# Decay attention and a gated projection on one core: other offsets of a list scheduler's priorities

## The chip, the cores and the metric

The kernel runs on 1 core of one Trainium2 chip. The metric is the device time of one execution in microseconds (us); a row of runs is told by its median. Three runs of the kernel before took 592.39, 594.8 and 597.3 us, the median is 594.8 us.

## What is computed

Eight batches of eight heads, 576 positions, head width 64. The result of the attention, heads side by side, is the x (576 x 512 for a batch) of a gated projection.

```python
scores = q @ k.T / sqrt(64)
cum    = cumsum(log(clip(f, 1e-4, 1)))
scores = where(causal, -1e9, scores + cum[:, None] - cum[None, :])
attn   = softmax(scores)                    # 1e-9 is added to the row sums
x      = attn @ v                           # heads side by side: 576 x 512 a batch
gate   = sigmoid(sum(conv_w[k] * x shifted by 4 - k rows, k = 0..4))
out    = (gate * (x @ w_val)) @ w_out
```

q, k, v and f are float32; the three weights are float64, which the kernel takes as pairs of 32-bit words and splits itself into a high and a low float part.

## The kernel before

**Units of work.** The 64 heads are done as 32 pairs i = 0..31, two heads in one unit, four pairs to a batch. A pair goes through these steps, and each step has a class name in the planner, which the text below uses:

- load, dec: DMAs of q, k, v and of the decay rows (tiles dm and dl); sel (L428, L431): GpSimd sets the causal part in them.
- T(i,q), T(i,k), T(i,z) (L524, L531): TensorE transposes q, k and the last 64 positions of both (z) into PSUM. The first four pairs copy the result as it is (TF, tile Xf, which lies in the tile named gate); from pair 4 on it is split into a high part (TH, tile Xh, L369) and a low part (TL, tile Xl, L515, always VectorE).
- S(i,...) (L354): the score products, in three groups. S(i,0) and S(i,1) fill four and two PSUM banks with rows 0 to 511 of both heads, S(i,z) fills two banks with rows 512 to 575. A group needs both parts of its transposes.
- red (L598): VectorE adds the decay in place and takes the row minimum; SX (L602): ScalarE takes the exponential into P or Pl and the row sums; rec (L611, L612): VectorE takes their reciprocals; norm: P or Pl is scaled, on GpSimd or VectorE (L376) or ScalarE (L374).
- PT (L643, L661, L662): TensorE transposes P, one unit for each head and group of row blocks; PT(i,l) is that of Pl. Copies bring the results into pt (L369).
- PV(i,0), PV(i,1) (L354, pt with vt): the products with v. Their result is copied to x (L369), and from x come xh (L369) and xl (L712), the two parts of x for the projection, and the five taps of the gate's convolution (conv: L376 or L374 for the first, L724 for four).

At the end of a batch follow sig (L740: sigmoid of the gate over 2304 columns, with a table load before and after it on ScalarE), Mv (x times w_val), H (L769), hh and hl (the two parts of the product), Mo(b,t) (times w_out, row block t of batch b) and O, OD (copy to ot and store). Each product of split operands is three matmuls. The eight blocks of 128 rows of the two weights, wv0 to wv3 and wo0 to wo3, are loaded into ot or wu and decoded during pairs 1 to 7 by some nine steps for each block: L822 to L834 on ScalarE and VectorE, a copy of the high part (L369 into wall) and a product for the low part (L862 into wall), which VectorE or GpSimd may do.

**What sets the order.** No order is written by hand. `plan_t`, `plan_s`, `plan_pt`, `plan_pv`, `plan_moe`, `plan_w` and `load` hand nodes to the class `Plan`: a class, the engines that may do the work with an assumed duration for each, what is read and written, and a base priority that is the pair's number plus a fraction. `Plan.add` adds to it OFF[class][phase], where the phase is 0 to 5 by the base priority (limits 0.95, 3, 6, 11, 28). `Plan.order` then simulates the engines with these durations: it takes the node that can start first (on an engine of several, its start plus PEN[class, engine][phase]), among those that can start at the same time the lowest priority. On TensorE a node of the same row layout as the one before is preferred by STICK. A node that needs PSUM takes from 8 banks the first that is free (`seize`, `room`), and a bank comes free when its last reader is done. What comes out is one fixed order of instructions for each engine and one fixed owner after another for each bank; on the chip the engines follow it with semaphores. So a number in the three tables moves an instruction on its own engine, gives an instruction to another engine, or gives a step another PSUM bank, and with it another predecessor to wait for.

## Time and profile before

| | |
|---|---|
| three runs | 592.39, 594.8, 597.3 us, median 594.8 |
| the profiled execution | 592.27 us, of it 590.5 us span from the first to the last instruction |
| TensorE busy | 558.2 us, 95% of the span |
| VectorE, ScalarE, GpSimd busy | 461.3, 447.9, 249.9 us |
| mean granted TensorE clock | 0.977 |
| DMA | 93.43 MB, 158 GB/s on average |

The profile is that of one execution. Its first part gives the busy time of each engine: PE is TensorE's matrix products, PEld its weight loads (which lie beside the products), DVE is VectorE, ACT ScalarE, POOL GpSimd, SP the queue that issues DMAs. Its second part cuts the span into 40 slices of 14.8 us. A row of a timeline gives the start, the time from the first start to the last end, the engine, the line in the kernel, the operation with the tile written and the tiles read, and how many instructions the row holds; in brackets stands the idle time of the engine ahead of the row and what ended it. A row of the windows gives a stretch and the busy time of PE, PEld, DVE, ACT and POOL in it, then the granted clock, the share of the DMA engines' time and GB/s. A row of the groups by line gives the count, then the busy time and the mean duration of one in ns, then the idle time ahead.

### The profile page before, as it was taken

To read this page: it belongs to the slowest core of one execution; us is meant where nothing else is said; L and a number is where in the kernel's file an instruction comes from. 1 tells how busy PE (TensorE), PEld (TensorE's weight loads), DVE (VectorE), ACT (ScalarE), POOL (GpSimd) and SP (SyncE) were. 2 spreads that over 40 slices of the span, in tenths; PEclk is the share of its full clock that TensorE was granted. 3 is DMA by queue.
4 is the path that set the end of the run, shared out by engine and by line. 5 is a ranking of instruction groups with operands and counts; after the bars stand their busy time and mean duration, and the time that the engine had idled before them with its cause. 6 is when DMAs were issued, how large, how long until landed. Compare 5 with 4: busy or idle time off the path is not lost.

```text
span 590.5 us, 14025 instructions
## 1 busy us (share of the span) xinstructions
PE 558.2 (95%) x4693; PEld 487.5 (83%) x4693; DVE 461.3 (78%) x1238; ACT 447.9 (76%) x1217; POOL 249.9 (42%) x398
## 2 busy tenths in 40 slices
PE   8778898799889999999999999999999999999997
PEld 7546587689779998889989988899888987889885
DVE  6488979899988797788967897668879789587660
ACT  4688878999878887888887988677798876764511
POOL 3431367334322556456553746455556461210200
PEclk9779699899999999999999999999999999999999
DMA  6979898676465585757866675466776544220012
GB/s 147 266 185 266 170 240 230 166 196 168 114 183 135 143 234 158 188 136 188 188 157 167 184 189 154 117 179 152 193 201 188 159 120 123 80 83 19 37 37 89
DMA packets 136294, 93.43 MB, mean 158 GB/s; under 512 B 118474, under 2 KB 118494, under 8 KB 136222
## 3 DMA queue, kind: packets, MB, share of 16 engines
q1 hardware_dynamic: 136142, 92.52, 59.0%
q8 instruction: 37, 0.61, 0.4%
q14 instruction: 35, 0.29, 0.2%
q10 hardware_dynamic: 80, 0.02, 0.0%
HBM read 82.60 MB, written 9.91 MB: 157 GB/s over the span
## 4 chain that ended last, share of the span: by engine, by line
PE 69%; DVE 13%; DMA 8%; ACT 5%; issue 3%; SPq 1%; POOL 1%; DVEq 0%; POOLq 0%; ACTq 0%
PE banks L354 54%; PE banks L643 9%; DVE banks L598 6%; PE banks L524 3%; DMA wu<-in_moe_w_val_dram 3%; ACT P L602 3%; DMA dm<-decd 2%; DVE gate L724 2%; PE banks L661 2%; DMA qn<-in_q_dram 1%; DVE negm L598 1%; SPq L381 1%; DMA kn<-in_k_dram 1%; PE banks L531 1%; ACT P L374 1%
## 5 line engine op out<-in xcount | busy, mean ns | idle before, releaser
L602 ACT ACTIVATE P<-banks,negm 128x256 f32<-128x256 f32 (+3 forms) x256 | 131.9, 531 | 35.9 <-DVE negm L598 35.6
L369 ACT COPY pt<-banks 128x256 f32<-128x256 f32 (+2 forms) x320 | 116.9, 436 | 42.8 <-PE banks L643 36.4
L598 DVE CUSTOM_DVE_ANT_0 banks<-banks,dm 128x256 f32<-128x256 f32 (+3 forms) x256 | 120.4, 515 | 33.4 <-PE banks L354 22.2
L724 DVE SCALAR_TENSOR_TENSOR gate<-x,cw,gate 128x576 f32<-128x576 f32 x128 | 111.6, 876 | 1.7
L354 PE MATMUL banks<-xh,wall 128*128 128x288 f32 x512 | 110.2, 300 | 1.0 <-ACT ot L369 0.7
L428 POOL TENSOR_SCALAR_AFFINE_SELECT dm<-dm 128x256 f32<-128x256 f32 x126 | 57.5, 481 | 122.0 <-DMA dm<-decd 100.1
L376 POOL TENSOR_SCALAR P<-P,rz 128x128 f32<-128x128 f32 (+3 forms) x132 | 79.0, 614 | 56.5 <-DVE rz L612 32.7
L643 PE MATMUL banks<-ident,P 128*128 128x128 f32 x640 | 93.2, 283 | 9.3 <-POOL P L376 4.1
L354 PE MATMUL banks<-pt,vt 128*64 128x128 f32 (+2 forms) x1408 | 99.0, 294 | 3.2 <-DVE Xl L515 1.9
L354 PEld LDWEIGHTS banks<-pt,vt 128*64 128x64 f32 x1408 | 87.1, 139 | 16.0 <-issue 3.1
L354 PE MATMUL banks<-wall,hh 128*128 128x512 f32 x288 | 92.8, 403 | 2.8 <-ACT P L602 2.6
L643 PEld LDWEIGHTS banks<-ident,P 128*128 128x128 f32 x640 | 74.4, 144 | 20.0 <-POOL P L376 5.3
L354 PEld LDWEIGHTS banks<-xh,wall 128*128 128x128 f32 x512 | 83.8, 188 | 2.8 <-ACT ot L369 1.1
L354 PE MATMUL banks<-xl,wall 128*128 128x288 f32 x256 | 75.4, 294 | 0.0
L712 POOL TENSOR_TENSOR xl<-x,xh 128x576 fp32r<-128x576 f32 x32 | 47.1, 1475 | 46.1 <-ACT xh L369 46.1
L354 PEld LDWEIGHTS banks<-wall,hh 128*128 128x128 f32 x288 | 51.0, 188 | 13.3 <-ACT P L602 3.6
L354 PE MATMUL banks<-Xh 128*128 128x288 f32 (+2 forms) x280 | 59.1, 346 | 1.2 <-DVE Xl L515 1.0
L782 POOL TENSOR_TENSOR hl<-h,hh 128x576 fp32r<-128x576 f32 (+2 forms) x36 | 36.9, 1032 | 48.4 <-ACT hh L369 48.4
L354 PE MATMUL banks<-wall,hl 128*128 128x512 f32 x144 | 56.5, 392 | 0.0
L354 PE MATMUL banks<-Xh,Xl 128*128 128x288 f32 (+2 forms) x280 | 53.6, 315 | 0.0
L354 PE MATMUL banks<-Xl,Xh 128*128 128x288 f32 (+2 forms) x280 | 53.3, 314 | 0.0
L602 ACT ACTIVATION_READ_ACCUMULATOR P<-banks,negm 128x1 f32 x256 | 52.9, 206 | 0.0
(105 smaller groups left out, 916.7 us busy)
## 6 DMA issues: line engine op xcount, KB each, us to landing
dm<-decd SPq DMA_DIRECT2D x62, 640.0 KB, 5.4
out_dram<-ot SPq DMA_DIRECT2D x36, 256.0 KB, 2.1
dl<-decd SPq DMA_DIRECT2D x62, 144.0 KB, 3.8
qn<-in_q_dram SPq DMA_DIRECT2D x64, 128.0 KB, 3.6
kn<-in_k_dram SPq DMA_DIRECT2D x64, 128.0 KB, 5.8
vt<-in_v_dram SPq DMA_DIRECT2D x64, 128.0 KB, 2.9
zn<-in_k_dram SPq DMA_DIRECT2D x32, 32.0 KB, 3.1
vt<-in_v_dram SPq DMA_DIRECT2D x32, 32.0 KB, 3.2
```

The costliest lines, as they stand in the source:

```text
L354: nc.tensor.matmul(out, lhsT=lhsT, rhs=rhs, start=start, stop=stop)
L369: (eng.copy if eng is nc.scalar else eng.tensor_copy)(out=out, in_=in_)
L376: eng.tensor_scalar(out=out, in0=in_, scalar1=col, scalar2=0.0, op0=ALU.mult, op1=ALU.add)
L428: nc.gpsimd.affine_select(out=t, in_=t, pattern=[[0, 2], [-1, P]], base=0, channel_multiplier=1, compare_op=ALU.is_ge, fill=-BIG)
L524: nc.tensor.transpose(out=bank(key)[:, n * P:(n + 1) * P], in_=src[:, n].rearrange("p h d -> p (h d)"), identity=ident)
L598: nc.vector.tensor_tensor_reduce(out=sl, in0=sl, in1=add[:, o:o + ext], op0=ALU.add, op1=ALU.min, scale=-0.125, scalar=3.0e38, accum_out=n ...
L602: nc.scalar.activation(out=dst[:, o:o + ext], in_=bank(key)[:, c0:c0 + ext], func=AF.Exp, bias=negm[r][:, col], scale=-1.0, accum_out=zs[r ...
L643: nc.tensor.transpose(out=bank(key)[:, c:c + P], in_=Pt[m][:, BOFF[b] + P * j:BOFF[b] + P * j + P], identity=ident)
L661: nc.tensor.transpose(out=bank(key)[:, P * j:P * j + P], in_=Pl[r][:, D + P * j:D + P * j + P], identity=ident)
L712: any_("xl", {"POOL": 1.4, "DVE": 0.67}, p, lambda eng: eng.tensor_tensor(out=xl[s], in0=xv, in1=xh[s][:, :].bitcast(F32), op=ALU.subtract ...
L724: eng.scalar_tensor_tensor(out=gt, in0=src, scalar=wt_, in1=gt, op0=ALU.mult, op1=ALU.add)
L782: eng.tensor_tensor(out=hl[jj][:, y:y + x1 - x0], in0=h32[:, x0:x1], in1=hh[jj][:, y:y + x1 - x0].bitcast(F32), op=ALU.subtract)
```

## The change

STICK goes from 18.18 to 16.65, and nearly all numbers of the tables OFF and PEN change; all steps, durations, buffers and dependencies stay. The new numbers come from the same kind of search as the old ones, with disturbances of the assumed durations half as large. Some rows of the diff:

```diff
-STICK = 18.18
+STICK = 16.65
...
-    ... "T": (25.97, 49.19, -30.29, -36.4, -10.95, -19.47),
+    ... "T": (13.33, 44.36, -9.43, -41.78, -1.47, -41.3),
...
-    ("norm", "ACT"): (0.44, 0.25, 1.01, 0.21, 1.1, 2.13),
+    ("norm", "ACT"): (0.0, 0.17, 13.52, 0.11, 0.94, 4.26),
...
+    ("wo", "POOL"): (0.0, 0.0, 0.13, 0.0, 0.0, 0.0), ...
```

What it does to the program, by the orders of the two kernels: the 3941 matmuls are the same, with 160 changes of row layout instead of 159. Of the norms, ScalarE has 118 instead of 100, VectorE 35 instead of 39, GpSimd 135 instead of 149. Of the eight low products of the weights (L862) VectorE has seven instead of four: wv0, wv2 and wo3 come to it from GpSimd. One first conv (pair 4) goes from ScalarE to VectorE, and one copy of a z transpose too. Three places follow that the prediction speaks of; the names at the end of a tile's name are its buffer.

TensorE, pairs 2 to 4 (kn_76 and zn_78 are k and z of pair 5, Pl_86 and the pt tiles those of pair 2, gate_114 the operands of S(3,1)). Before:

```order
L643 MATMUL banks<-ident,P_84 128x128 x4
L524 MATMUL banks<-ident,kn_76 128x128 x4
L354 MATMUL banks<-gate_114 128x384 x2
L354 MATMUL banks<-gate_114 128x128 x2
L643 MATMUL banks<-ident,P_85 128x128 x4
L531 MATMUL banks<-ident,zn_78 128x128 x2
L661 MATMUL banks<-ident,Pl_86 128x128 x4
L662 MATMUL banks<-ident,Pl_86 64x128
L354 MATMUL banks<-pt_89,vt_91 64x128
```

Now, from the last product of PV(2,0) on:

```order
L354 MATMUL banks<-pt_90,vt_91 64x128
L661 MATMUL banks<-ident,Pl_86 128x128 x4
L662 MATMUL banks<-ident,Pl_86 64x128
L524 MATMUL banks<-ident,kn_76 128x128 x4
L531 MATMUL banks<-ident,zn_78 128x128 x2
L354 MATMUL banks<-pt_89,vt_91 64x192
```

PV(2,0), the rows of pt with 64x128, stood behind T(5,k), S(3,1), T(5,z) and PT(2,l); now it stands ahead of T(5,k), T(5,z) and PT(2,l), and right behind S(3,1); PV(2,1), the rows with 64x192, follows T(5,z), and S(4,z), which stood between PV(2,0) and PV(2,1), follows PV(2,1) and the first transposes of pair 3.

TensorE, pairs 3 to 6 (qn_73, kn_75 and zn_77 are q, k and z of pair 6; P_83 and P_85 are P of pair 4, Xh_80 and Xl_82 the operands of S(5,...)). Before, behind S(4,1):

```order
L354 MATMUL banks<-Xl_81,Xh_79 128x128 x2
L524 MATMUL banks<-ident,qn_73 128x128 x4
L524 MATMUL banks<-ident,kn_75 128x128 x4
L531 MATMUL banks<-ident,zn_77 128x128 x2
L643 MATMUL banks<-ident,P_84 128x128 x4
```

Now, inside the products of pair 5:

```order
L354 MATMUL banks<-Xl_82,Xh_80 128x256 x2
L643 MATMUL banks<-ident,P_83 128x128 x2
L643 MATMUL banks<-ident,P_85 128x128 x4
L524 MATMUL banks<-ident,kn_75 128x128 x4
L531 MATMUL banks<-ident,zn_77 128x128 x2
L354 MATMUL banks<-Xh_80 128x384 x2
L354 MATMUL banks<-Xh_80,Xl_82 128x384 x2
```

T(6,k) and T(6,z) stood right behind T(6,q), ahead of PT(3,1,(2,0)); T(6,q) has stayed there, T(6,k) and T(6,z) now follow PV(3,0), PV(3,1), S(5,z), PT(4) and S(5,0).

VectorE, the last weight block wo3 (gate_114 holds the parts being decoded, wu the block; dm_68 and dm_69 are the decay tiles of pair 9). Before:

```order
L832 SCALAR_TENSOR_TENSOR gate_114<-wu 128x512
L834 TENSOR_SCALAR wu<-gate_114 128x512
L369 CAST wall<-gate_114 128x512
L598 ISA banks,negm_94<-banks,dm_68 128x512
L598 ISA negm_94 128x1
L598 ISA banks,negm_94<-banks,dm_69 128x512
```

Now:

```order
L832 SCALAR_TENSOR_TENSOR gate_114<-wu 128x512
L834 TENSOR_SCALAR wu<-gate_114 128x512
L369 CAST wall<-gate_114 128x512
L862 TENSOR_TENSOR wall<-gate_114,wu 128x512
L376 TENSOR_SCALAR gate_114<-x_99,cw 128x576
L376 TENSOR_SCALAR gate_114<-x_100,cw 128x576
L598 ISA banks,negm_94<-banks,dm_68 128x512
```

The low product of wo3 (L862) has come to VectorE, and two first taps of the convolution stand behind it, ahead of the row minima of pair 9.

One more place, in words: on TensorE the first row block of the output product, Mo(0,2) and Mo(0,3) of batch 0 (L354, wall with hh and hl), stood behind PT(8,1,(2,0)) and PT(8,l); now both stand ahead of them, and Mo(0,2) has a bank that PT(8,0,(2,0)) leaves where before it had one that S(9,1) leaves, while Mo(0,3) now has one of S(9,1). On ScalarE the sigmoid of batch 1's gate with its table loads now stands ahead of the pt copies of pair 8.

More of the change, by code (lines that the diff above doesn't have):

```diff
@@ L63 @@
 }
 PEN = {
[4 rows of a table removed]
-    ("X", "DVE"): (10.66, 6.42, 35.96, 35.67, 3.07, 32.37), ("conv", "ACT"): (37.06, 9.53, 0.39, 7.85, 12.52, 8.12),
-    ("conv", "DVE"): (0.01, 0.0, 0.02, 0.0, 0.09, 1.39), ("conv", "POOL"): (51.47, 31.7, 58.49, 34.72, 29.95, 35.69),
-    ("hh", "ACT"): (0.0, 0.0, 0.0, 0.0, 0.5, 3.04), ("hh", "DVE"): (0.0, 0.0, 1.73, 16.52, 3.91, 0.39),
-    ("hl", "DVE"): (0.0, 0.0, 0.45, 0.87, 4.98, 0.0), ("hl", "POOL"): (0.0, 0.0, 0.0, 0.67, 0.0, 30.02),
-    ("load", "ACT"): (1.58, 0.0, 0.0, 0.0, 0.0, 0.0), ("norm", "ACT"): (0.44, 0.25, 1.01, 0.21, 1.1, 2.13),
@@ L74 @@
-    ("norm", "DVE"): (6.2, 19.99, 21.87, 2.29, 2.56, 0.18), ("norm", "POOL"): (0.63, 17.37, 0.04, 25.85, 0.46, 2.15),
-    ("sel", "DVE"): (36.1, 36.18, 41.87, 17.73, 90.83, 1.24), ("sel", "POOL"): (0.65, 0.76, 0.61, 0.6, 1.44, 6.22),
-    ("start", "ACT"): (10.22, 0.0, 0.0, 0.0, 0.0, 0.0), ("start", "DVE"): (4.31, 0.0, 0.0, 0.0, 0.0, 0.0),
-    ("start", "POOL"): (5.56, 0.0, 0.0, 0.0, 0.0, 0.0), ("wo", "ACT"): (0.0, 0.0, 5.81, 0.0, 0.0, 0.0),
[4 rows of a table removed]
[4 rows of a table added]
+    ("conv", "ACT"): (37.96, 19.77, 7.45, 24.88, 23.07, 22.76), ("conv", "DVE"): (0.12, 0.0, 0.02, 0.0, 0.08, 1.2),
@@ new lines @@
+    ("conv", "POOL"): (46.14, 15.26, 57.23, 24.18, 25.57, 24.33), ("cut0", "ACT"): (0.18, 0.0, 0.0, 0.0, 0.0, 0.0),
+    ("hh", "ACT"): (0.0, 0.0, 0.0, 0.0, 0.5, 20.58), ("hh", "DVE"): (0.0, 0.0, 3.69, 4.33, 8.35, 0.06),
+    ("hl", "DVE"): (0.0, 0.0, 0.34, 5.33, 13.61, 0.3), ("hl", "POOL"): (0.0, 0.0, 0.19, 0.21, 0.13, 30.97),
+    ("load", "ACT"): (2.24, 0.0, 0.0, 0.0, 0.0, 0.0), ("norm", "ACT"): (0.0, 0.17, 13.52, 0.11, 0.94, 4.26),
+    ("norm", "DVE"): (11.52, 23.51, 21.54, 13.3, 3.63, 0.16), ("norm", "POOL"): (0.05, 12.7, 0.04, 30.93, 0.45, 2.7),
@@ L82 @@
+    ("sel", "DVE"): (32.07, 32.67, 50.11, 9.42, 80.65, 0.16), ("sel", "POOL"): (1.41, 0.6, 0.06, 0.1, 0.26, 18.53),
+    ("start", "ACT"): (14.6, 0.0, 0.0, 0.0, 0.0, 0.0), ("start", "DVE"): (2.21, 0.0, 0.0, 0.0, 0.0, 0.0),
+    ("start", "POOL"): (3.01, 0.0, 0.0, 0.0, 0.0, 0.0), ("wo", "ACT"): (0.0, 0.0, 16.48, 0.0, 0.0, 0.0),
[4 rows of a table added]
 }
```

10 lines of the change are left out of this document (5 added, 5 removed), and 44 rows, old and new, of tables (OFF, PEN).

## The prediction

> **What bounds the kernel now.** I read the page's first two parts, then the windows by stage, then the waits in the timelines of PE, DVE and POOL, then the chain that ended last.
>
> ```profile
> span 590.5 us, 14025 instructions
> PE 558.2 (95%) x4693; PEld 487.5 (83%) x4693; DVE 461.3 (78%) x1238; ACT 447.9 (76%) x1217; POOL 249.9 (42%) x398
> ...
> PEclk9779699899999999999999999999999999999999
> ```
>
> PE is busy for 558.2 of 590.5 us and does the same 3941 matmuls afterwards. An order alone can win only the 32.3 us in which PE stands still and what PE loses at a lower clock; it can lose without such a limit. The clock row has its low digits in the first eight slices (14.8 us each). Where the idle time lies, the windows tell:
>
> ```profile
> core 0: us, PE busy (x) PEld busy (x) DVE busy (x) ACT busy (x) POOL busy (x), PEclk, DMA share, GB/s
> 15.00:45.00 30.00, 22.00 (x135) 15.57 (x134) 18.77 (x55) 21.51 (x59) 12.59 (x21) 0.77 0.91 226
> 60.00:75.00 15.00, 12.42 (x68) 9.12 (x66) 13.26 (x36) 12.10 (x37) 5.67 (x8) 0.67 0.77 163
> 90.00:170.00 80.00, 70.86 (x612) 61.38 (x611) 75.36 (x199) 72.00 (x195) 33.06 (x47) 0.98 0.63 171
> 170.00:300.00 130.00, 129.50 (x1170) 117.02 (x1169) 106.79 (x288) 109.24 (x300) 65.37 (x106) 1.00 0.68 176
> 300.00:590.00 290.00, 283.44 (x2395) 251.88 (x2394) 211.48 (x562) 200.54 (x538) 115.26 (x170) 1.00 0.47 130
> ```
>
> From 170 us on PE itself is the bound: 0.50 us idle of 130, then 6.56 of 290. Between 90 and 170 us PE is idle for 9.14 us, and DVE, busy for 75.36 of 80, is the bound. Between 15 and 45 us PE is idle for 8.00 us, and the DMA engines are busy at 0.91. Whatever the new order does after 170 us can hardly gain; what it does earlier has to pass DVE or the DMAs.
>
> **The start, pairs 0 and 1 (term A).** GpSimd's norms of pair 0 end PE's longest wait.
>
> ```profile
> 22.29 2.85 PE L643 MATMUL banks<-ident,P 128*128 128x128 f32 x12 [3.45 <-POOL P L376]
> ```
> ```profile
> 21.01 0.77 POOL L428 TENSOR_SCALAR_AFFINE_SELECT dm<-dm 128x256 f32<-128x256 f32 x2 [4.41 <-DMA dm<-decd]
> ```
>
> POOL stood 4.41 us in front of a select that waited for its DMA, with the norms queued behind it; the new order puts two of these norms ahead of the select and gives ScalarE norms of pair 1. At best the whole wait of 3.45 us goes. But the next thing that all else waits for is a weight block, in the chain that ended last:
>
> ```profile
> 39.33 8.42 DMA wu<-in_moe_w_val_dram
> ...
> 54.10 7.02 DMA wu<-in_moe_w_val_dram
> ```
>
> The blocks of 512 KB take 8.42 and 7.02 us while the DMA engines are 0.91 busy, and the second waits for wu until the first is decoded. Work of pairs 0 and 1 that ends earlier then waits longer at 47.75 us. A DMA share of 0.91 is nearest to "no gain": I take 0, bounds -3.45 and 0.
>
> **Pairs 2 to 4 (term B).** The first order fence. DVE's waits here:
>
> ```profile
> 75.77 0.77 DVE L598 CUSTOM_DVE_ANT_0 banks<-banks,dl 128x576 f32<-128x576 f32 x1 [1.25 <-PE banks L354]
> ...
> 78.36 0.52 DVE L376 TENSOR_SCALAR gate<-x,cw 128x576 f32<-128x576 f32 x1 [1.55 <-ACT x L369]
> ...
> 80.22 0.70 DVE L598 CUSTOM_DVE_ANT_0 banks<-banks,dm 128x512 f32<-128x512 f32 x1 [0.49 <-PE banks L354]
> ```
>
> DVE waits 1.25 us for S(4,z), 1.55 us for the x of pair 2 and 0.49 us for S(4,0), 3.29 us together. PE loses this beside them:
>
> ```profile
> 64.56 0.79 PE L524 MATMUL banks<-ident,kn 128*128 128x128 f32 x4 [1.45 <-ACT P L602]
> ...
> 71.51 2.83 PE L354 MATMUL banks<-pt,vt 128*64 128x128 f32 x24 [0.71 <-ACT P L602]
> ```
>
> T(5,k) waits 1.45 us for a PSUM bank that an exponential of pair 3 holds, with everything behind it, and PV(2,0) 0.71 us. With PV(2,0) ahead of T(5,k), its bank from a copy of PT(2), PE has work during the 1.45 us, and PV(2,1), now ahead of S(4,z), brings x earlier: the 1.55 goes. S(4,z) and S(4,0), on the other hand, stand behind more transposes, so the 1.25 and the 0.49 stay or grow. DVE is busy for 13.26 of 15 us in this window, so what it can win is bounded by its waits: bounds -3.3 and 0. About half of the 3.29 belongs to the wait that goes: -1.6.
>
> **Low products, a conv and a cast on DVE (term C).**
>
> ```profile
> L862 POOL TENSOR_TENSOR wall<-gate,ot 128x512 fp32r<-128x512 f32 x3 | 4.0, 1335 | 3.9 <-DVE ot L834 3.9
> L862 DVE TENSOR_TENSOR wall<-gate,wu 128x512 fp32r<-128x512 f32 x3 | 2.1, 684 | 0.0
> ...
> L376 DVE TENSOR_SCALAR gate<-x,cw 128x576 f32<-128x576 f32 x31 | 16.7, 540 | 14.5 <-ACT x L369 14.5
> ```
>
> Three low products at 0.684 us are 2.05 us more for DVE (3 x 1.335 less for POOL, which has 47 of 80 us free), the first conv is 0.54; the cast of a z transpose (0.34 us, row at 90.19 below) and one step of the table's start that goes to ScalarE cancel nearly. Together at most +2.7. wv0 and wv2 fall into stretches in which DVE waits for DMAs (the 1.26 us ahead of 47.77 below) and cost nothing there; wo3 falls between 154 and 156 us in DVE's bound stretch, ahead of pair 9's row minima:
>
> ```profile
> 47.77 0.43 DVE L824 TENSOR_SCALAR gate<-wu 128x512 int32<-128x512 int32 x1 [1.26 <-DMA wu<-in_moe_w_val_dram]
> ```
>
> I take +0.7, the one product that has no cover, bounds 0 and +2.7 (all cover gone).
>
> The Trainium skill speaks against this: "GPSIMD Engine Reference", section "1. Specifications", has GpSimd share its SBUF interface with VectorE, so that VectorE instructions with two SBUF inputs contend with it. These rows show that it matters here:
>
> ```profile
> 155.48 0.69 DVE L598 CUSTOM_DVE_ANT_0 banks<-banks,dm 128x512 f32<-128x512 f32 x1
> ...
> 158.36 7.51 DVE L724 SCALAR_TENSOR_TENSOR gate<-x,cw,gate 128x576 f32<-128x576 f32 x7
> ...
> 167.57 0.81 DVE L724 SCALAR_TENSOR_TENSOR gate<-x,cw,gate 128x576 f32<-128x576 f32 x1
> ```
> ```profile
> 155.31 1.40 POOL L862 TENSOR_TENSOR wall<-gate,wu 128x512 fp32r<-128x512 f32 x1 [3.81 <-DVE wu L834]
> ...
> 161.92 3.34 POOL L712 TENSOR_TENSOR xl<-x,xh 128x576 fp32r<-128x576 f32 x2 [4.93 <-ACT xh L369]
> ```
>
> Seven convs beside two of POOL's xl took 7.51 us where one alone takes 0.81, so 1.84 us were lost in POOL's 3.34. But the row minimum that ran beside POOL's product of wo3 took 0.69 us, as the one at 80.22 did (0.70). By that rule the move would give back up to 1.40 x 1.84 / 3.34 = 0.77 us and term C would be about 0, the sum 0.7 lower; by the row beside this very product there is nothing to give back, and I stay with +0.7.
>
> **Mo(0,2) (term D).**
>
> ```profile
> 167.91 0.72 PE L354 MATMUL banks<-wall,hh 128*128 128x512 f32 x2 [2.40 <-ACT P L602]
> ```
>
> Mo(0,2) waits 2.40 us for a bank that the exponentials of S(9,1) leave, and these wait for DVE, which does the seven convs first (7.51 us, above). Now Mo(0,2) takes a bank that a copy of PT(8,0) leaves, but Mo(0,3) behind it takes one of S(9,1), and PT(8,1) and PT(8,l), now behind both, take banks that T(11,q) and T(11,k) leave; and on ScalarE the sigmoid comes ahead of the copies of PT(8):
>
> ```profile
> 170.05 1.28 ACT L740 ACT_TABLE_LOAD   x1
> 171.35 2.13 ACT L740 ACTIVATE gate<-gate 128x2304 f32<-128x2304 f32 x1
> 173.50 1.28 ACT L742 ACT_TABLE_LOAD   x1
> ```
>
> That is 4.69 us in which no copy for PV(8) is made. So Mo(0,2)'s 1.4 us of work come earlier and the same wait stands in front of Mo(0,3): the bounds are -2.40 and 0, and I take -0.5, near the lower gain since the releaser (S(9,1)) is the same.
>
> **After 170 us (term E).** PE is 99.6% and 97.7% busy there, the reorders of pairs 10 to 30 move work that is covered: 0. The bounds are -2 (of 7.06 us idle) and +2, a wait like that of 2.40 above where a bank's new owner is late. In the last batch the order at the end is the old one.
>
> **The sum.** 0 - 1.6 + 0.7 - 0.5 + 0 = -1.4, by which the profiled execution of 592.27 (span 590.5, 1.8 around it) would take 590.9. That execution was 2.5 us below the median of the three runs shown; against it the forecast is 594.8 - 1.4 = 593.4 us. 1% of the median, about what a measurement of this kernel can tell from no change, is 5.9 us: faster means below 588.9, slower above 600.7.
>
> **Rival 1, faster: the early clock comes back.** Between 60 and 75 us the clock was 0.67: PE lost up to 15 x (1 - 0.67) = 4.95 us. If the earlier PV(2,0) fills T(5,k)'s wait and PE stays at full clock, the gain is 4.95 + 1.45 + 0.71 = 7.1, so 585.2 against the profile and 587.7 against the median. For it: the order does just that, and PE's low clock makes every step in the window longer. Against it: DVE is busy for 13.26 of the 15 us there, so that only 1.74 can be taken out of this window before DVE binds. Chance 0.25.
>
> A page bears on how far the clock would come back: "TensorE: Matmul & The Clock Gate", section "What's actually happening", of the Trainium skill has the clock halved after at least one idle window of about 3.4 us. Taken literally, no wait of the 60 to 75 us stretch could have halved it. This trace does not agree with the literal reading:
>
> ```profile
> 105.00:120.00 15.00, 11.59 (x101) 10.38 (x98) 13.43 (x35) 14.94 (x39) 2.88 (x7) 0.89 0.58 159
> ```
> ```profile
> 108.47 0.66 PE L524 MATMUL banks<-ident,kn 128*128 128x128 f32 x4 [2.19 <-ACT P L602]
> ```
>
> Here the clock was 0.89 with waits of at most 2.19 us. By the rule the rival's gain would be 1.45 + 0.71 = 2.2, that is 592.6; by the rows it is 7.1, and the rival goes by the rows.
>
> **Rival 2, slower: T(6,k) comes too late.** The second order fence.
>
> ```profile
> 88.87 0.68 DVE L369 CAST Xh<-banks 128x512 fp32r<-128x512 f32 x1
> 89.58 0.69 DVE L515 TENSOR_TENSOR Xl<-banks,Xh 128x512 fp32r<-128x512 f32 x1
> 90.19 0.34 DVE L369 CAST Xh<-banks 128x192 fp32r<-128x192 f32 x1
> 90.57 0.36 DVE L515 TENSOR_TENSOR Xl<-banks,Xh 128x192 fp32r<-128x192 f32 x1
> ...
> 100.12 0.76 DVE L598 CUSTOM_DVE_ANT_0 banks<-banks,dl 128x576 f32<-128x576 f32 x1
> ```
> ```profile
> 81.68 0.60 PE L524 MATMUL banks<-ident,kn 128*128 128x128 f32 x4
> ...
> 98.02 0.40 PE L354 MATMUL banks<-Xh 128*128 128x288 f32 x1
> ```
>
> The last split of pair 6's z ended at 90.93, S(6,z) started at 98.02: 7.1 us of cover. T(6,k) and T(6,z) now run some 8 us later on PE (from 81.68 to about 90, by the work that now stands ahead: PV(3), S(5,z), PT(4) and half of S(5)), and their two casts and two low parts (0.68 + 0.69 + 0.34 + 0.36 = 2.07) go between the row minima of pair 5, in a stretch in which DVE has no slack. If that 2.07 delays the minima of S(5,1), and with them the exponentials, PT(5) and S(6), and all 2.7 of term C has to be paid there, and the wait costs clock as at 105 to 120 us (15 x (1 - 0.89) = 1.65), the change costs 6.4: 598.7 against the profile, 601.2 against the median. It decides once the split of z ends behind S(6,z)'s turn on PE. For it: the cover is used up. Against it: DVE does the same work in total, only later, and the minimum of S(6,z) stood behind other DVE work until 100.12 in any case. Chance 0.13.
>
> **Rival 3: all of it is absorbed.** The two stretches before 170 us stay bound by DVE and by the weight DMAs, B and D find the next wait at once: 594.8, with a chance of 0.07. The forecast has 0.55.
>
> **How the numbers follow.** Rival 1 lies below 588.9: faster 0.25. The forecast and rival 3 lie within 1%: 0.62. Rival 2 lies above 600.7: 0.13. The forecast's own range is 590 to 598 (the terms' bounds halved, with the run-to-run spread of 592.39 to 597.30). The range reaches to rival 1 and beyond it by half of A's bound, and to rival 2: 585.5 to 601.
>
> **What would show it.** A: the wait of 3.45 us at PT(0) is shorter, but the first weight block of the chain still ends near 47.7. B: T(5,k)'s wait of 1.45 is gone, PV(2,0) starts before 71.5 relative to S(3,1), DVE's 1.55 ahead of the first conv is below 0.8; if the clock in 60 to 75 us is above 0.85, rival 1 holds. C: DVE busy time rises by 2 to 3 us, and nothing else of it shows. D: the 2.40 stands in front of Mo(0,3) or PT(8,1) instead. Rival 2 shows as a wait of PE on DVE's Xl ahead of S(6,z), near 98 us. The forecast is wrong if more than 6 us are won or lost, above all if they appear after 170 us, where I priced nothing.

## The result and the profile after

The changed kernel took 598.94 us (median of 19 runs, 595.89 to 603.23), the kernel before 595.17 us (19 runs, 591.51 to 600.41): ratio 1.0066, 95% interval 1.0042 to 1.0090, so 3.9 us slower. The forecast was 593.4 us, 1.4 us faster. The profiled execution of the changed kernel took 599.67 us (span 597.8), that of before 592.27 (span 590.5). The two profiles thus lie 7.4 us apart where the ratio gives 3.9: about half of what they differ by is chance, and a stretch of one profile alone proves little.

The page of the changed kernel, its first two parts:

```profile
span 597.8 us, 14007 instructions
PE 556.7 (93%) x4693; PEld 483.0 (81%) x4693; DVE 467.4 (78%) x1238; ACT 453.1 (76%) x1234; POOL 240.3 (40%) x381
...
PEclk9897999999999999999999999999999999999999
```

PE is busy for 556.7 us (558.2 before): the time was lost in idle PE, 41.1 us of the span after 32.3. The clock is no cause: it has fewer low digits than before, and the mean granted clock is 0.991 where it was 0.977. The same windows as before the change:

```profile
core 0: us, PE busy (x) PEld busy (x) DVE busy (x) ACT busy (x) POOL busy (x), PEclk, DMA share, GB/s
15.00:45.00 30.00, 22.39 (x162) 16.22 (x160) 20.90 (x65) 24.07 (x69) 9.95 (x19) 0.94 0.91 251
60.00:75.00 15.00, 12.05 (x101) 8.68 (x102) 14.23 (x40) 13.45 (x40) 4.31 (x9) 1.00 0.61 167
90.00:170.00 80.00, 69.56 (x604) 60.55 (x603) 76.09 (x194) 69.61 (x184) 32.07 (x43) 1.00 0.66 178
105.00:120.00 15.00, 10.19 (x93) 8.54 (x92) 13.85 (x37) 13.96 (x39) 2.07 (x6) 1.00 0.70 171
170.00:300.00 130.00, 127.55 (x1151) 113.53 (x1149) 103.97 (x274) 108.41 (x305) 67.24 (x103) 1.00 0.63 165
300.00:590.00 290.00, 285.10 (x2393) 251.66 (x2392) 217.40 (x570) 205.64 (x553) 107.76 (x159) 1.00 0.47 131
```

The row to look at is 170 to 300 us: PE stands for 2.45 us there, after 0.50 before, and it begins 1151 matmuls in the 130 us instead of 1170. The prediction had called this stretch covered.

### The profile page after: what moved, and what is told of

Same layout as the page of the kernel before. It is cut to its first block, busy times and chain, and to the rows that moved or that the text cites. A ratio compares the mean times of both kernels' runs of the same rounds, so it can differ in the third digit from the quotient of the medians.

```text
span 597.8 us, 14007 instructions
## 1 busy us (share of the span) xinstructions
PE 556.7 (93%) x4693; PEld 483.0 (81%) x4693; DVE 467.4 (78%) x1238; ACT 453.1 (76%) x1234; POOL 240.3 (40%) x381
## 4 chain that ended last, share of the span: by engine, by line
PE 52%; DVE 21%; ACT 11%; DMA 8%; issue 4%; SPq 2%; POOL 1%; DVEq 0%; POOLq 0%; ACTq 0%
PE banks L354 41%; DVE banks L598 7%; PE banks L643 7%; DVE gate L724 6%; ACT P L602 6%; DMA dm<-decd 3%; SPq L381 2%; ACT pt L369 2%; DMA dl<-decd 2%; PE banks L524 2%; DVE negm L598 1%; DVE Xh L369 1%; DMA zn<-in_k_dram 1%; DMA wu<-in_moe_w_val_dram 1%; PE banks L661 1%
## 5 line engine op out<-in xcount | busy, mean ns | idle before, releaser
L602 ACT ACTIVATE P<-banks,negm 128x512 f32<-128x512 f32 (+3 forms) x256 | 131.9, 529 | 43.7 <-DVE negm L598 43.5
L598 DVE CUSTOM_DVE_ANT_0 banks<-banks,dm 128x512 f32<-128x512 f32 (+3 forms) x256 | 120.1, 514 | 28.0 <-PE banks L354 16.9
L369 ACT COPY pt<-banks 128x256 f32<-128x256 f32 (+2 forms) x320 | 115.2, 438 | 31.3 <-PE banks L643 28.6
L724 DVE SCALAR_TENSOR_TENSOR gate<-x,cw,gate 128x576 f32<-128x576 f32 x128 | 114.9, 902 | 1.8
L354 PE MATMUL banks<-xh,wall 128*128 128x288 f32 x512 | 110.6, 301 | 2.4 <-ACT pt L369 0.9
L354 PE MATMUL banks<-pt,vt 128*64 128x128 f32 (+2 forms) x1408 | 99.3, 295 | 6.9 <-DVE Xl L515 4.0
L354 PEld LDWEIGHTS banks<-pt,vt 128*64 128x64 f32 x1408 | 87.5, 139 | 20.1 <-ACT pt L369 5.1
L376 POOL TENSOR_SCALAR P<-P,rz 128x128 f32<-128x128 f32 (+3 forms) x120 | 72.0, 613 | 71.0 <-DVE rz L612 20.5
L643 PE MATMUL banks<-ident,P 128*128 128x128 f32 x640 | 91.2, 279 | 6.8 <-POOL P L376 4.1
L354 PE MATMUL banks<-wall,hh 128*128 128x512 f32 x288 | 92.9, 403 | 0.6 <-ACT pt L369 0.6
L354 PEld LDWEIGHTS banks<-xh,wall 128*128 128x128 f32 x512 | 83.8, 188 | 5.2 <-ACT pt L369 1.4
L643 PEld LDWEIGHTS banks<-ident,P 128*128 128x128 f32 x640 | 72.5, 141 | 18.3 <-POOL P L376 5.3
L354 PE MATMUL banks<-xl,wall 128*128 128x288 f32 x256 | 75.6, 295 | 1.2 <-POOL xl L712 1.2
L712 POOL TENSOR_TENSOR xl<-x,xh 128x576 fp32r<-128x576 f32 x32 | 48.2, 1506 | 54.2 <-ACT xh L369 31.0
L354 PE MATMUL banks<-Xh 128*128 128x288 f32 (+2 forms) x280 | 59.8, 347 | 2.8 <-ACT P L602 1.1
L354 PEld LDWEIGHTS banks<-wall,hh 128*128 128x128 f32 x288 | 50.9, 188 | 10.7 <-ACT pt L369 1.5
L354 PE MATMUL banks<-wall,hl 128*128 128x512 f32 x144 | 56.5, 392 | 0.0
L374 ACT ACTIVATE P<-P,rz 128x384 f32<-128x384 f32 (+3 forms) x105 | 54.2, 565 | 1.8 <-DVE rz L612 1.8
L354 PE MATMUL banks<-Xh,Xl 128*128 128x288 f32 (+2 forms) x280 | 53.7, 314 | 0.0
L354 PE MATMUL banks<-Xl,Xh 128*128 128x288 f32 (+2 forms) x280 | 53.4, 313 | 0.0
L602 ACT ACTIVATION_READ_ACCUMULATOR P<-banks,negm 128x1 f32 x256 | 52.4, 205 | 0.0
```

What stands on the lines that cost most here:

```text
L354: nc.tensor.matmul(out, lhsT=lhsT, rhs=rhs, start=start, stop=stop)
L369: (eng.copy if eng is nc.scalar else eng.tensor_copy)(out=out, in_=in_)
L374: eng.activation(out=out, in_=in_, func=AF.Copy, scale=col)
L376: eng.tensor_scalar(out=out, in0=in_, scalar1=col, scalar2=0.0, op0=ALU.mult, op1=ALU.add)
L598: nc.vector.tensor_tensor_reduce(out=sl, in0=sl, in1=add[:, o:o + ext], op0=ALU.add, op1=ALU.min, scale=-0.125, scalar=3.0e38, accum_out=n ...
L602: nc.scalar.activation(out=dst[:, o:o + ext], in_=bank(key)[:, c0:c0 + ext], func=AF.Exp, bias=negm[r][:, col], scale=-1.0, accum_out=zs[r ...
```

## Where the two orders part

Windows by the clock compare different work. The two orders agree in what PE does for short pieces near 101 to 135, 178 to 206, 277, 416 and 506 to 540 us, and a tile that starts there is the same point of the program in both. By the start times of such tiles on PE (timelines, in us; the pieces are named by the first tile behind the cut) the span falls into six segments (the last one ends at one of PE's last products, 6.6 us ahead of the end of the span in both):

```
                     to PT(6,0)  to PV(9,0)  to PV(14,0)  to T(26,q)  to PT(29,0)  to the end
before                  121.6       69.7         84.4        138.2        92.6        77.4
after                   121.3       68.9         87.1        140.3        95.2        78.3
```

The third segment, near 190 to 277 us, costs 2.7 us more; the later ones 2.1, 2.6 and 0.9 more; what comes first gains about 1. This is one execution each. Whether it holds, and by what mechanism, the experiments ask.

## The experiments: which stretch costs time

The first runs join the two tables. The kernel carries both sets and toggles between them at a number of units of work on PE, at places where the orders agree; all steps and durations stay. The edit, once for all:

```diff
+OFF2 = {...}   PEN2 = {...}
+SWAP = (216,)
...
-prio=prio + OFF.get(cls, NONE)[phase(prio)]
+prio=prio + OFF.get(cls, NONE)[phase(prio)], prio2=prio + OFF2.get(cls, NONE)[phase(prio)]
...
+two = sum(units >= k for k in SWAP) % 2
-cand.append((t + pen, nd["prio"] - ...
+cand.append((t + pen, (nd["prio2"] if two else nd["prio"]) - ...
...
+units += e == "PE"
```

OFF2 and PEN2 are the new numbers. SWAP = (0, 216) has the new order up to PV(9,0) and the old one after it, (216,) the reverse. STICK, the third thing in the diff, needs no run: the order comes out the same with 18.18 and with 16.65 (all the joined kernels keep 18.18, and in each segment PE does the same as in the kernel whose tables hold there).

**New order up to 190 us** (SWAP = (0, 216)):

> The scheduler carries both sets of tables and changes from the one to the other at a count of TensorE units at which both orders agree: here the new tables hold for the first 216 units (to about 205 us of the span), the old ones for the rest, so that the program is word for word the changed one before the splice and the old one behind it. Theory 1 (the loss lies late: many small waits on TensorE behind 190 us, where it is the bound; in the two profiles the changed kernel is 1.1 us ahead at 190 us and 7.2 behind at the end): this kernel is 0.5 to 2 us faster than the kernel before, ratio 0.996 to 0.999, and its profile shows PV(9,0) about 1 us earlier than before. Theory 2 (the loss lies in the first 190 us, and the profile of before only drew a good execution): it carries the whole loss, ratio 1.005 to 1.009.

Measured: 592.12 us, ratio 0.9974 [0.9938, 1.0010]: 1.5 us less by the ratio, not told from no change.

**New order from 190 us on** (SWAP = (216,)):

> The converse: old tables for the first 216 TensorE units, the new ones behind. Theory 1: all of the loss and none of the gain, 4 to 8 us slower than before, ratio 1.007 to 1.013, the profile 7 to 9 us longer from PV(9,0) to the end than that of before. Theory 2: no change, ratio 0.998 to 1.002.

Measured: 601.8 us, ratio 1.0118 [1.0066, 1.0171], that is 7.0 us more. So the loss lies behind PV(9,0), in what the prediction put down as term E with nothing.

**New order from 190 to 277 us alone** (SWAP = (216, 312)):

> New tables only for TensorE units 216 to 312 (about 205 to 277 us), the old ones ahead and behind. Theory 1: this piece has 2.7 us of the profile's late loss of 8.3, so 1.5 to 3 us slower than before, ratio 1.002 to 1.005. Theory 2: no change, ratio 0.998 to 1.002.

Measured: 596.66 us, ratio 1.0062 [1.0031, 1.0093], 3.7 us more: this one stretch, with the old order ahead of it and behind it, costs about as much as the whole change.

**New order from 277 to 416 us alone** (SWAP = (312, 496)):

> New tables only for TensorE units 312 to 496 (about 277 to 416 us). Theory 1: this piece has 2.0 us of the profile's late loss, so 1 to 2 us slower than before, ratio 1.002 to 1.004; what is then left, 2.7 us between 416 and 506 us and 0.8 at the end, is in no run of this call alone. Theory 2: no change, ratio 0.998 to 1.002.

Measured: 595.55 us, ratio 1.0028 [1.0002, 1.0054]: 1.7 us more, barely told from none.

**Inside the early part**: SWAP = (126, 216), near 125 to 190 us, and SWAP = (0, 126), up to there:

> New tables only for TensorE units 126 to 216 (about 130 to 205 us; the two orders agree between units 101 and 135, and between 182 and 222), the old ones ahead and behind. Theory 1a (the early gain is made behind 100 us: in the five profiles so far the stretch from S(6,0) to Mv(1,0) takes 77.6 to 79.4 us in the old order and 75.1 and 73.9 in the new, with the wait of Mo(0,2) gone, while the first 100 us take 98.3 to 101.4 old and 97.5 and 102.1 new): 2 to 5 us faster than before, ratio 0.992 to 0.997, and the stretch from Mv(0,2) to Mv(1,0) at least 2 us shorter, above all by the 2.4 us at Mo(0,2). Theory 1b (the gain is made in the first 100 us, by PV(2,0) moved ahead): no change, 0.998 to 1.002.

Measured: 594.63 us, ratio 1.0016 [0.9986, 1.0046].

> New tables only for the first 126 TensorE units (to about 130 us). Theory 1a: no gain or up to 1.5 us slower, ratio 0.998 to 1.003. Theory 1b: the whole early gain, 1.5 to 3 us faster, ratio 0.995 to 0.998.

Measured: 594.14 us, ratio 1.0026 [0.9996, 1.0056]. Neither the gain nor the loss that was looked for in the early part is told from nothing. The profiles say why it can't be: up to PT(6,0) executions of these kernels took 116.7 to 124.4 us, without regard to the order that they had there.

The segments of these profiles, with the order of each (o old, n new):

```
                 PT(6,0)     PV(9,0)     PV(14,0)    T(26,q)     PT(29,0)     end
s_early_new      116.7 n     67.6 n      84.5 o      139.2 o     93.9 o       77.4 o
s_late_new       122.8 o     70.6 o      86.0 n      139.7 n     94.3 n       78.2 n
s_third_new      123.0 o     70.7 o      86.1 n      139.5 o     95.7 o       77.4 o
s_fourth_new     119.1 o     69.7 o      84.3 o      139.0 n     94.8 o       77.5 o
s_second_new     124.4 o     67.3 n      84.7 o      139.0 o     94.3 o       77.5 o
s_first_new      123.9 n     69.0 o      84.3 o      138.9 o     92.9 o       77.8 o
```

The third segment is steady: 84.3 to 84.7 us in the five executions with the old order, 86.0 to 87.1 in the three with the new one. So 1.7 us or a little more is a property of the order, and here its cause can be sought. The second segment is 67.3 and 67.6 us with the new order and 69.0 to 70.7 with the old one in these six; what became of that gain stands under term D. Behind 277 us the orders overlap: 139.0 to 140.3 against 138.2 to 139.5, 94.3 and 95.2 against 92.6 to 95.7; only the last segment is apart, 78.2 and 78.3 against 77.4 to 77.8. The times of s_late_new (+7.0) and s_third_new (+3.7, interval 1.8 to 5.5) are more than these profiles show by segments (1.7 to 2.7 in the third, under 1 in the last); the rest is not located.

## The experiments: by what mechanism

In the third segment PE loses little in waits that the profile shows. The row of that window, before, and s_third_new:

```profile
191.30:275.70 84.40, 83.90 (x762) 75.50 (x761) 67.51 (x183) 69.70 (x193) 48.15 (x80) 1.00 0.67 178
```
```profile
193.70:279.80 86.10, 85.09 (x762) 75.47 (x761) 69.15 (x185) 68.71 (x192) 49.91 (x78) 1.00 0.66 172
```

PE has 762 matmuls in both. It is idle for 1.01 us instead of 0.50, and busy for 1.19 more: the profile models the ends of matmuls, so a short wait between two of them can show as a longer matmul and not as idle time. That this is what the 1.19 us are is a reading; no run shows it. DVE is busy for 1.64 us more with two instructions more. ScalarE's waits in that stretch (columns: us in total, times, longest us), of before, of the change, and of s_third_new:

```profile
ACT P L602 <- DVE negm L598: 4.9, 7, 1.2
ACT Pl L602 <- DVE negm L598: 2.6, 3, 1.2
```
```profile
ACT P L602 <- DVE negm L598: 8.0, 6, 2.5
ACT Pl L602 <- DVE negm L598: 0.9, 1, 0.9
```
```profile
ACT P L646 <- DVE negm L642: 8.7, 7, 2.4
```

(L646, L642, L768 and L756 of the joined kernels are L602, L598, L724 and L712.) The exponentials into P wait 3 to 4 us longer in all for the row minima, with one wait of 2.4 that was not there; those into Pl wait 1.7 us less, so that 1.4 to 2.1 us remain. Two theories were held, one after the other, for what that does and where it is from. By **theory W**, ScalarE's late exponentials keep PSUM banks, and the new order's choice of which tile follows in which bank turns this into waits of PE. By **theory P**, which came up only after the runs with other banks, VectorE is late itself, because a convolution tap ran beside GpSimd.

**Less work for ScalarE.** The exponentials and norms of pairs 10 and later take half of their columns, so part of the softmax is left out; with the old order, and with the new one from 190 to 277 us:

```diff
-def ex(key=keys[n], col=col, c0=c0, ext=ext, ...
+def ex(key=keys[n], col=col, c0=c0, ext=ext // 2 if i >= 10 else ext, ...
-sl = (Pt[m] if u < 2 else Pl[m])[:, o:o + ext]
+sl = (Pt[m] if u < 2 else Pl[m])[:, o:o + (ext // 2 if i >= 10 else ext)]
```

> The old order, with the exponentials and the norms of pairs 10 to 31 done for the left half of their columns only (the right half of P and Pl is left as it was, so the output is not that of the reference). It is the base for the next run. The stretch from PV(9,0) to PV(14,0), 84.3 to 84.5 us so far in the old order, should lose its three waits (0.42, 0.33 and 0.19 us), of which two are for exponentials: 83.4 to 84.2 us.

Measured: 587.37 us in one execution; third segment 84.0.

> The same halved exponentials and norms with the new tables for TensorE units 216 to 312, where the new order takes 86.0 to 87.1 us from PV(9,0) to PV(14,0) against 84.3 to 84.5. Theory W (the loss is made of waits for PSUM banks that exponentials and copies on ScalarE still hold: 0.41 at T(14,k), 0.53 to 0.66 at PV(11,0), 0.17 and 0.46 at S(14,0), 0.20 at PT): with short exponentials these waits go, and the stretch is at most 0.7 us longer than in the halved old order. Theory K (the loss comes from the sequence of unit kinds itself, more changes between products of different shape): the difference stays at 1.5 us or more.

Measured: 589.70 us in one execution; third segment 83.5 us: the excess of 1.7 over the old order is gone (-0.5). That is the number of theory W. But the run does not tell the two theories apart, nor does it show that the loss goes through ScalarE: the halved work has also moved what theory P is about. DVE and POOL of s_half_third where the late tap is looked for below:

```profile
222.11 1.02 DVE L768 SCALAR_TENSOR_TENSOR gate<-x,cw,gate 128x576 f32<-128x576 f32 x1
```
```profile
222.49 1.93 POOL L756 TENSOR_TENSOR xl<-x,xh 128x576 fp32r<-128x576 f32 x1
```

The tap, which takes 2.06 us at this place in s_third_new, takes 1.02 here, and GpSimd's xl, which starts 0.38 us behind it, is the longer one; the next such tap takes 1.61 us instead of 2.06.

**Other banks, same order.** All units of work stay in their place, only the PSUM bank that each tile gets is written over after the order is made, such that tiles follow in banks that came free earlier:

```diff
+HOMES = ("5630256715324016352401637452603751460275...", ...)
...
-for fn, e in plan.order(BEGIN):
+steps = list(plan.order(BEGIN))
+for key, n in zip(plan.home, HOMES):
+    plan.home[key] = [int(n) + k for k in range(plan.width[key])]
+for fn, e in steps:
```

> The order with the new tables for TensorE units 216 to 312 only, word for word on every engine; but after the planning the PSUM banks are given out anew (a table of one digit for each owner), so that more time lies between the last reader of a bank and its next owner. Theory W (the late loss is made of waits for PSUM banks that ScalarE still reads): the waits of 0.41 at T(14,k), 0.53 to 0.66 at PV(11,0), 0.17 and 0.46 at S(14,0) go, and the stretch from PV(9,0) to PV(14,0) falls from 86.0 to 87.1 us to 84.9 or less. Theory E (the exponentials and the copies themselves come too late, since ScalarE has more or other work, and whoever needs their data waits): the stretch stays at 85.7 us or more.

Measured: 590.29 us in one execution, but third segment 86.4 us: not shorter. PE's waits for banks went to other places, the longest in front of a product that had none:

```profile
251.57 0.40 PE L408 MATMUL banks<-Xh 128*128 128x288 f32 x1 [1.45 <-ACT pt L423]
```

As a matter of the owners of banks theory W falls for this stretch, as far as the one other table of owners can tell: the stretch is no shorter with it, and PE now waits for ScalarE's pt copies.

> The changed kernel's order with the banks given out anew. Theory W: behind 190 us the waits of TensorE for ScalarE (about 8 us in the changed kernel's profile, about 2.5 in that of before) fall below 3 us, and the kernel is 3 to 6 us faster than the changed one, so about as fast as the one before: ratio to before 0.996 to 1.002. Theory E: no change against the changed kernel, ratio to before 1.004 to 1.009.

Measured, with the new order all through: 599.37 us, ratio 1.0084 [1.0044, 1.0124]; third segment 87.1 as with the planner's own banks. Behind 277 us this profile is 7.2 us shorter than that of the change (306.6 and 313.8), where the median of the whole is no shorter; what banks do there is not decided.

> The order of the kernel before with the banks given out anew. Theory W: its own waits for banks go too, 2.41 us at Mo(0,2), 1.45 at T(5,k), 1.6 to 2.5 at T(8,k), 0.42 at Mo(1,4), so 2 to 6 us faster than before, ratio 0.990 to 0.997: then this is the faster order of the two. Theory E: no change, ratio 0.998 to 1.002.

Measured, with the old order: 589.89 us, ratio 0.9909 [0.9871, 0.9947], 5.4 us **faster** than before, and so faster than both kernels; third segment 82.9 us. The 2.40 us of PE at Mo(0,2) are gone. The same stretch of its waits, 160 to 180 us, before and with other banks:

```profile
PE banks L354 <- ACT P L602: 2.4, 1, 2.4
```
```profile
PE banks L408 <- ACT P L656: 0.3, 1, 0.3
PE banks L408 <- ACT pt L423: 0.2, 1, 0.2
```

So other owners are worth time in the old order, where the third segment of the new one gained nothing by them. (L408, L656 and L423 here are L354, L602 and L369.)

**What keeps VectorE.** DVE, POOL and ACT of s_third_new near 225 us:

```profile
225.24 2.06 DVE L768 SCALAR_TENSOR_TENSOR gate<-x,cw,gate 128x576 f32<-128x576 f32 x1
227.22 0.69 DVE L642 CUSTOM_DVE_ANT_0 banks<-banks,dm 128x512 f32<-128x512 f32 x1
...
227.83 0.72 DVE L642 CUSTOM_DVE_ANT_0 banks<-banks,dm 128x512 f32<-128x512 f32 x1
```
```profile
225.25 1.43 POOL L756 TENSOR_TENSOR xl<-x,xh 128x576 fp32r<-128x576 f32 x1
```
```profile
228.00 0.69 ACT L646 ACTIVATE P<-banks,negm 128x512 f32<-128x512 f32 x1 [2.41 <-DVE negm L642]
...
232.14 0.70 ACT L413 COPY x<-banks 128x384 f32<-128x384 f32 x2
232.71 1.65 ACT L413 COPY pt<-banks 128x512 f32<-128x512 f32 x4
```

A convolution tap and GpSimd's subtraction xl = x - xh start within 0.01 us of each other, and the tap takes 2.06 us. The row minima of the next scores stand right behind it, the first exponential waits 2.41 us for them, and in ScalarE's queue the copies of x and pt stand behind eight exponentials. The same happens near 249 us (a tap of 2.06 us, and an exponential waits 2.00 us). The changed kernel has it too, DVE and POOL:

```profile
222.42 2.07 DVE L724 SCALAR_TENSOR_TENSOR gate<-x,cw,gate 128x576 f32<-128x576 f32 x1
224.41 0.69 DVE L598 CUSTOM_DVE_ANT_0 banks<-banks,dm 128x512 f32<-128x512 f32 x1
```
```profile
222.44 1.43 POOL L712 TENSOR_TENSOR xl<-x,xh 128x576 fp32r<-128x576 f32 x1
```

Before, the same xl ran beside the second and third row minimum, which did not mind; DVE and POOL:

```profile
225.34 0.70 DVE L598 CUSTOM_DVE_ANT_0 banks<-banks,dm 128x512 f32<-128x512 f32 x1 [2.78 <-PE banks L354]
...
225.95 0.73 DVE L598 CUSTOM_DVE_ANT_0 banks<-banks,dm 128x512 f32<-128x512 f32 x1
...
226.60 0.47 DVE L598 CUSTOM_DVE_ANT_0 banks<-banks,dm 128x256 f32<-128x256 f32 x1
```
```profile
226.01 1.43 POOL L712 TENSOR_TENSOR xl<-x,xh 128x576 fp32r<-128x576 f32 x1
```

Between 170 and 300 us no tap of before took over 1.3 us; in the changed kernel four did, 1.87 to 2.07 us. As to the two near 222 and 247 us, it is the order that decides: they take 1.71 to 2.07 us in all five profiles with the new order there and all of the work (two of them with other banks), and no tap between 210 and 280 us is over 1.3 us in the six such profiles with the old order.

The planner does not see this clash. `Plan.order` has a rule against it: on VectorE an instruction of a class in PORT (the taps, class conv, are one) starts only when GpSimd's planned work is over, and the other way round (L41, L211, L251). In its simulation the tap and xl thus never overlap. On the chip nothing but each engine's own order and the data that an instruction needs holds them apart, and they meet.

**Without the subtraction.** Theory P says: take xl away and only the new order gains. For pairs 10 and later xl is not computed, so the second part of the split of x keeps old values there; the planner's order stays.

```diff
-any_("xl", {"POOL": 1.4, "DVE": 0.67}, p, lambda eng: eng.tensor_tensor(
+any_("xl", {"POOL": 1.4, "DVE": 0.67}, p, lambda eng: None if i >= 10 else eng.tensor_tensor(
```

> New tables for TensorE units 216 to 312 only, and the low parts of x (GpSimd's product in L712) left out for pairs 10 to 31, so that xl keeps older values and the output is not that of the reference. Everything else keeps its place. Theory P (GpSimd's xl stretches the convolution tap that stands in front of the row minima, ScalarE waits for the minima with its copies behind, TensorE waits for their banks): no tap above 1.3 us between 190 and 280 us, the two waits of ScalarE of 2.4 and 2.0 us shrink by over 1 us each, and the stretch from PV(9,0) to PV(14,0) falls from 86.1 to 85.0 us or less. Theory Q (the minima come late because the new order puts them behind more work on VectorE and their score products behind other units on TensorE): the stretch stays at 85.7 us or more.

Measured: 591.28 us in one execution; third segment 83.9 us, 2.2 less than with xl. DVE and ACT at the same place:

```profile
223.44 0.81 DVE L768 SCALAR_TENSOR_TENSOR gate<-x,cw,gate 128x576 f32<-128x576 f32 x1
224.21 0.70 DVE L642 CUSTOM_DVE_ANT_0 banks<-banks,dm 128x512 f32<-128x512 f32 x1
```
```profile
225.00 0.69 ACT L646 ACTIVATE P<-banks,negm 128x512 f32<-128x512 f32 x1 [1.29 <-DVE negm L642]
```

The tap is back at 0.81, the exponential's wait at 1.29, and that near 249 us at 0.74.

> The old order without the low parts of x for pairs 10 to 31, the base for the other two. It has no tap above 1.3 us between 170 and 300 us, so by both theories the stretch from PV(9,0) to PV(14,0) stays at 84.0 to 84.4 us.

Measured, old order: 592.73 us, ratio 0.9976 [0.9909, 1.0042]; third segment 84.4, as before.

> The changed kernel's order without the low parts of x for pairs 10 to 31. Theory P: from PV(9,0) to PV(14,0) 85.3 us or less instead of 87.1, and to PT(29) and the end less than 1.5 us longer than the next run altogether. Theory Q: 86.3 us or more there, and at least 3 us longer than the next run from PV(9,0) to the end.

Measured, new order all through: 592.28 us, ratio 0.9954 [0.9882, 1.0026]; third segment 84.4, 2.7 less than the change. Its row and that of the change:

```profile
191.10:275.40 84.30, 83.96 (x760) 75.64 (x759) 67.10 (x182) 69.52 (x194) 47.18 (x76) 1.00 0.67 175
```
```profile
190.20:277.30 87.10, 85.63 (x760) 75.58 (x759) 70.17 (x182) 69.45 (x194) 52.40 (x80) 1.00 0.67 170
```

With the same 182 instructions DVE is busy for 3.07 us less. Leaving out four subtractions of GpSimd takes 3.1 us off another engine, and 2.7 off PE's segment; in the old order it takes nothing. That is theory P. The whole kernels agree: against before, the new order is 0.9954 [0.9882, 1.0026] without xl and 1.0066 [1.0042, 1.0090] with it, and without xl its 592.28 us are not above the 592.73 of the old order. That is four executions each, though, with intervals as wide as the whole loss. Two things beside the taps go with xl. PE's products of x with the weights wait once for xl itself in the third segment of the change (0.3 us; 0.06 in s_third_new). And GpSimd's norms, which stand behind xl in its queue, come earlier; but no wait of PE in the third segment of the change or of s_third_new ended on a norm of GpSimd. Behind 277 us the two orders lie 1.4 us apart without xl (307.7 and 306.3) and 5.6 apart with it (313.8 and 308.2), in one profile each; since profiles with the old order there and all of the work take 308.2 to 312.7 us, what the new order costs there, and by what, stays open. Moving xl to another engine, or ahead of the tap, was not tried.

## Why the prediction was wrong, step by step

**Term E failed: "the reorders of pairs 10 to 30 move work that is covered: 0".** Measured +7.0 us for the order behind PV(9,0) alone (s_late_new) and +3.7 for its first 86 us alone (s_third_new); the first is beyond the bound of +2 with its whole interval, the second by its middle only (its interval begins at 1.8), and the sign of the whole change turns on them. PE's busy share of 99.6% was read as cover for everything else. It is none: it says that the other engines were in time in that order, not by how much. VectorE and ScalarE were busy for 0.82 and 0.84 of those 130 us, and two late taps ahead of row minima were enough to use up what slack they had (1.25 us each). The prediction said it would be wrong above all if a loss appeared after 170 us "where I priced nothing", and so it was.

**What the prediction had in hand and used for one place only.** In term C it quoted seven taps beside two xl (7.51 us where one alone takes 0.81). It weighed the rule of the Trainium skill, "GPSIMD Engine Reference", section "1. Specifications", that GpSimd shares its SBUF interface with VectorE and instructions with two SBUF inputs contend, and put it aside for the product of wo3, by the row of a row minimum. For that product it was right to: moved to VectorE it takes 0.68 us, and the row minimum behind it 0.69 as before. But the row that the prediction went by could not speak against the rule: a row minimum has one of its two inputs in PSUM, and none is stretched beside GpSimd in the rows shown here. DVE of the change:

```profile
155.03 0.68 DVE L862 TENSOR_TENSOR wall<-gate,wu 128x512 fp32r<-128x512 f32 x1
...
156.68 0.69 DVE L598 CUSTOM_DVE_ANT_0 banks<-banks,dm 128x512 f32<-128x512 f32 x1
```

But the rule holds for all taps of the program (2.06 and 2.07 us beside xl against 0.81 alone agree with it), and a new order of VectorE and GpSimd is a new draw of which of them meet. The prediction asked the question of one product and never of the taps of pairs 10 to 14.

**Term A (0): consistent.** The wait at PT(0) is 3.21 us (3.45 before), PE:

```profile
22.36 1.97 PE L643 MATMUL banks<-ident,P 128*128 128x128 f32 x8 [3.21 <-POOL P L376]
...
47.60 0.66 PE L661 MATMUL banks<-ident,Pl 128*128 128x128 f32 x4 [2.33 <-ACT P L602]
```

GpSimd's norm is hardly earlier, and near 47 us PE waits again. DVE waits for the weight block just ahead of that, as said (the block lands 1.4 us earlier than before, at 46.41 instead of 47.77):

```profile
46.41 0.43 DVE L824 TENSOR_SCALAR gate<-wu 128x512 int32<-128x512 int32 x1 [2.13 <-DMA wu<-in_moe_w_val_dram]
```

**Term B (-1.6): the signs came, the gain is not told from nothing.** PE from 67 to 71 us:

```profile
67.15 1.53 PE L354 MATMUL banks<-pt,vt 128*64 128x128 f32 x24 [0.91 <-ACT pt L369]
...
70.36 0.63 PE L524 MATMUL banks<-ident,kn 128*128 128x128 f32 x4 [0.98 <-issue]
```

PV(2,0) comes 4.4 us earlier by the clock, T(5,k)'s 1.45 is 0.98, and DVE's three waits (3.29 us) are gone (a fourth, of 0.88 us for an exponential, is now 0.65). Still PE is busy for 12.05 of the 15 us where it was 12.42. **Rival 1** had its sign, and as a property of the order: the clock between 60 and 75 us is 1.00 in the four profiles with the new order up to there and the planner's banks, 0.67 to 0.89 in nine with the old. Its 7.1 us did not come. Some of the clock is lost between 45 and 60 us instead, though not in every execution: it is 0.77, 0.77, 0.89 and 1.00 there in the four, 0.92 to 1.00 in the nine (before, then the change):

```profile
45.00:60.00 15.00, 12.63 (x105) 9.56 (x105) 13.52 (x40) 13.21 (x38) 3.06 (x7) 1.00 0.95 267
```
```profile
45.00:60.00 15.00, 10.35 (x78) 8.43 (x77) 10.94 (x29) 11.27 (x31) 3.74 (x6) 0.77 0.91 226
```

And the rest PE could not use: DVE is busy for 14.23 of the 15 us behind it, which is what the prediction had against this rival. Up to PT(6,0) the four took 116.7 to 123.9 us, the nine 119.1 to 124.4, and the order up to 125 us alone (s_first_new) is 1.0026 [0.9996, 1.0056].

**Term C (+0.7): its sign was not met, and its cost does not show.** DVE's busy time rose by 6.1 us, not by 2 to 3. The three low products are 2.05; the taps as a group went from 111.6 to 114.9 us, the first taps from 16.7 to 20.0:

```profile
L724 DVE SCALAR_TENSOR_TENSOR gate<-x,cw,gate 128x576 f32<-128x576 f32 x128 | 114.9, 902 | 1.8
L376 DVE TENSOR_SCALAR gate<-x,cw 128x576 f32<-128x576 f32 x32 | 20.0, 629 | 22.5 <-ACT x L369 22.4
```

The 3.3 us of the first group are the stretched taps: 128 in both kernels, a mean of 902 ns after 876. The first taps are one more, and longer (629 ns after 540); where they meet GpSimd was not followed up. The moved products themselves cost nothing that the runs show.

**Term D (-0.5): the place was right, the cause was not seen.** The wait of 2.40 at Mo(0,2) went and did not move to Mo(0,3) or PT(8,1), which have none. PE of the change:

```profile
164.80 0.70 PE L354 MATMUL banks<-wall,hh 128*128 128x512 f32 x2
...
170.37 0.60 PE L643 MATMUL banks<-ident,P 128*128 128x128 f32 x4
```

The 2.40, though, is not a property of the old order. In the profiles of nine kernels with the old order and the planner's banks there, it is 2.40 to 2.42 in five and 0.26 or 0.27 in four. Here are PE, DVE and POOL of one of the four, s_half_old, whose halved work comes only later:

```profile
165.20 0.73 PE L398 MATMUL banks<-wall,hh 128*128 128x512 f32 x2 [0.26 <-ACT P L646]
```
```profile
157.80 5.20 DVE L768 SCALAR_TENSOR_TENSOR gate<-x,cw,gate 128x576 f32<-128x576 f32 x7
```
```profile
161.36 4.28 POOL L756 TENSOR_TENSOR xl<-x,xh 128x576 fp32r<-128x576 f32 x2 [4.93 <-ACT xh L413]
```

It is the same clash again, with two outcomes: the seven taps take 7.51 us and the two xl 3.34 (the profile of before), or the taps 5.20 and the xl 4.28. Where the taps lose, the row minima of pair 9 are 2.3 us later, the exponentials too, and Mo(0,2) waits 2.1 us longer. So the prediction, which named the seven taps as what delays these exponentials, saw the chain but took one of its outcomes for the price. The second segment is 69.7 to 70.7 us in the five and 67.0 to 69.0 in the four, and 67.3 to 70.3 in four with the new order and the planner's banks; a gain of the order there is not shown. **Rival 2** was on the right side (601.2), but no wait of PE stands ahead of S(6,z) near 98 us, and the loss is not there.

The early terms together, -1.4, can't be held against s_early_new's -1.5, which is not told from none; what was taken as nothing behind them was the result.

## What to carry to other kernels

An engine that is 99% busy is no cover for a new order of the others: ask of each stretch which instruction it follows closest behind, and what may make that one late. Where two engines share a port, compare in the trace the same instruction alone and beside the other engine, and treat each new order as a new draw of their meetings, above all ahead of what a strict queue waits for. Take a change of order apart where the two orders agree, use a stretch that repeats within some tenths of a microsecond where the whole kernel scatters by several, and take no wait of a single profile for a property of the order.
